# Group 11's reciprocal real gate: from two ScalarE steps to one GpSimd power

## The chip, the cores and the metric

The kernel runs on one NeuronCore of a Trainium2 chip. Its engines are TensorE (PE in the profile: matrix products), VectorE (DVE) and ScalarE (ACT) for work on tiles in the on-chip memory, GpSimd (POOL), which does simple tile work and issues small DMAs in software, and SyncE (SP), which issues the large loads, stores and transposing DMAs. Every engine works through its own queue in order; semaphores hold an instruction until what it reads is there. The metric is the time of one execution in microseconds (us) on the device, lower is better.

## The reference

The reference is a gated linear recurrence, followed by a gated feed-forward layer with a residual. The part that matters here is the complex gate `a_re + i a_im` of each time step, head and channel, which is scaled to a magnitude of at most 0.999:

```python
mag = np.sqrt(a_re * a_re + a_im * a_im)
scale = np.minimum(mag, 0.999) / (mag + 1e-06)
a_re_n, a_im_n = (a_re * scale, a_im * scale)
for t in range(S):
    ar, ai = a_re_n[:, :, t, :, None], a_im_n[:, :, t, :, None]
    new_re = ar * S_re - ai * S_im
    new_im = ar * S_im + ai * S_re
    S_re, S_im = (new_re + kv, new_im)
    y[:, :, t] = np.einsum('bhd,bhde->bhe', q[:, :, t], S_re)
```

`kv` is the outer product of k and v at step t. There are 4 batches, 8 heads, 768 steps and 48 channels. After it, `x = y` reshaped to 3072 x 384 goes through `x + sigmoid(x @ w_res) * ((gelu(x @ w_gate) * (x @ w_val)) @ w_out)`, with 1536 hidden columns.

## The kernel before, in words

The recurrence is turned into a chunked form. The 768 steps of each batch are cut into three stretches of 256, each of two chunks of 128 steps; a stretch of one batch is a **group**, and there are 12 groups (0 to 3 are the first stretch of the four batches, 4 to 7 the second, 8 to 11 the third). Steps lie on the 128 partitions, heads and channels along the row, 384 numbers for a chunk and 768 for a group.

For each group the gate becomes two running sums over time: that of the logarithm of the magnitude, and that of the phase. The phase of a gate is arctan(a_im / a_re). So the kernel needs a_im times the reciprocal of a_re, which it takes as the square of a_re to the power -1/2. Steps are named with the group behind them; for group 11 they run so:

- SQI11 and SQR11 (ScalarE): squares of a_im and a_re, the latter in place in tile `ar`.
- ADD11 (VectorE, L573): adds both squares into tile `m2`, capped. It reads `ar`.
- LNR11 and EXR11 (ScalarE, L577 and L578): logarithm of `ar` in place, then its exponential with a scale of -0.5: now `ar` holds 1/a_re.
- TH11 (VectorE, L554): `ai` = `ar` times `ai`. ATN11 (ScalarE) is its arctangent.
- CST11.c (TensorE, L631): running sum of the phases of a chunk as a product with a triangular matrix, in f32.

A chunk's running phase has to begin where the chunk before it ended. The last row of the reduced phase is multiplied by -2 pi into a row of a scratch tile `G` (CRA and CRB steps, L679), and a DMA with accumulation adds it to the first row of the next chunk's `ai` (CDA and CDB steps, L684; GpSimd issues them). CDB4 carries from group 4's second chunk to group 8's first, and **CST8.0 on TensorE reads that row**; OFF8.0 on ScalarE reads CST8.0's result. The other small GpSimd DMAs move rows of the magnitudes through DRAM so that the state of the recurrence can be scaled (DR at L582, DS at L585, DE and DI, DT at L611). GpSimd also does casts of v (VC, L520) and additions of the residual (RX, L874).

The feed-forward layer works on units of 256 or 512 rows: products with the gate and value weights (L837), gelu (ScalarE), their product (VectorE, L848), the residual gate (L852), the output product (L862), and the rest on VectorE, GpSimd and SyncE. PSUM accumulators of the products and of the running sums share four banks, named in the order.

The order of all work is written out by hand in `ORDER`, one list of about 1370 steps. Each step goes to one engine, and each engine's queue has its steps in the order of the list; nothing is rearranged when the kernel runs. The names `log`, `trig` and `gelu` in it load ScalarE's function tables.

In that list, on GpSimd, the steps around the change are RX3.1, then CDB4, DS8.1, DS9.1, DR10, DR11, DI8, CRA9, CDA9 and DT8.0. LNR11 stood between RX3.1 and CDB4 in the list, but on ScalarE's queue; EXR11 stood shortly before TH11.

Of the kernel before, what the change touches and what calls it, by code (L numbers as in the profile page):

```python
# [10 lines left out]
FP = mybir.dt.float32  # L11
# [3 lines left out]
OP = mybir.AluOpType  # L15
PSUM = bass.MemoryType.PSUM

PARAMS = {'units': [[0], [1], [2], [3], [4, 5], [6, 7], [8, 9], [10, 11]],
 'turn': 5,
 'wq': 4,  # L20
 'split': [0],
 'bufs': {'ar': 4,
          'ai': 6,
          'm2': 4,
          'q': 4,
          'k': 4,
# [235 lines left out]
        'XC4.0': 'ACT',  # L262
        'XC4.1': 'DVE'},
 'pairf': 1,
 'rat': []}

ORDER = """
# [46 lines left out]
DE6:1 GP4.0:2 Lai10.1 QT6:1 SQI11:1 SG4.3 GP4.3:3 VP4.11:1 GE4.3 SQR11 RX2.0 Lvf6.1:1 GE4.0 KR7 VP4.5:0 HM4.11 MM7:1  # L314
MN7 EN7 GP4.9:3 RP4.2:1 SQI10:2 DK6.0 SG4.2 GE4.9 HM4.5 ADD11 CSL9.0:211 VP4.3:0 ADD10 KT6:1 AT6.0.1:10 HM4.3 DS9.0:0
DE7:0 RX3.0 DS8.0:1 log EI9.0 CDB5 CSL8.0:100 CST9.0:3 AT6.0.0:01 EX9.0 CSL8.1:0 VC7.0:0 EX8.0 RX3.1 AM6.0.1 AM6.0.0
EI8.0 VC6.1 EX8.1 LNR11 CDB4 DS8.1 MI6:1 DS9.1 OFF9.0 CST8.0:2 DR10:0 ST2.0 DR11:1 DI8 Y6.0:3 FR9.0 AT6.1.1:10
AT6.1.0:01 AM6.1.1 DK6.1 ED6 EI8.1 AM6.1.0 OFF8.0 CRA9 CSL9.1:1 VP4.10:3 VP4.1:0 EI9.1 X6.0 ST3.0 Lvf7.1:0 EX9.1 LM10
LM11 ML8 LNR10 ML9 FR8.0 ME8 Y6.1:5 X6.1 EB7:0 EXR11 EXR10 QT7:0 HM4.10 HM4.1 KT7:0 AT7.0.1:10 AT7.0.0:01 CDA9 AM7.0.0
VP4.6:1 Lk10.0:3 Lq11.0:2 Lk8.0:2 VP4.0:2 VP4.9:3 VP4.8:0 HM4.6 AM7.0.1 HM4.0 CST9.1:1 HM4.9 OFF9.1 TH11 FR9.1 DT8.0:0  # L320
VP4.4:2 RP4.0:3 Y7.0:4 DK7.0 HM4.4 HM4.8 AT7.1.0:00 VC7.1 CRA8 CDA8 RP4.1:1 XD6.1:1 AT7.1.1:11 CST8.1:2 AM7.1.0 MI7:1
ST3.1 XD6.0 OFF8.1 FR8.1 AM7.1.1 OP4.0.0:0 trig ATN11 Lk8.1 Lvf8.1:1 X7.0 gelu SG4.0 Lq9.1:1 ABS9 OT4.0:2 Lvf9.0:0
# [56 lines left out]
def kernel(  # L379
# [13 lines left out]
    nc = tc.nc  # L393
    B, H, S, D = q.shape
    DD = 2 * D
    DM = H * D
# [15 lines left out]
    singles = ctx.enter_context(tc.tile_pool(name="singles", bufs=1))  # L412
# [4 lines left out]
    if PARAMS["rat"]:  # L417
        one = singles.tile([128, 1], FP, name="one")
        nc.vector.memset(one, 1.0)
    lmat, tmat = [], []  # L420
    for val, dst in ((1.0, lmat), (I2PI, tmat)):
        ut = singles.tile([128, 128], FP, name="ut%d" % (val == 1.0))
# [79 lines left out]
    def flat(t):  # L502
        return t.rearrange("p c h d -> p (c h d)") if len(t.shape) == 4 else t

    def part(key, cs):
        return flat(st[key])[:, cs[0] * DM:(cs[-1] + 1) * DM]

    def act(out, in_, func, **kw):
        return nc.scalar.activation(out=out, in_=in_, func=func, **kw)  # L509

    def on(name, default):
        return PARAMS["eo"].get(name, default)
# [14 lines left out]
    def gates(p):  # L527
        s = p // B
        split = p in PARAMS["split"]
        parts = [(0,), (1,)] if split else [(0, 1)]  # L530

        def each(nm, eng, f, r, w, table=None, whole=False):
            for cs in ([(0, 1)] if whole else parts):
                name = nm + str(p) + ("" if len(cs) > 1 else ".%d" % cs[0])
                e = on(name, eng)
                st.add(name, e, (lambda cs=cs, e=e: f(cs, e)) if nm in ("SQI", "SQR") else lambda cs=cs: f(cs),
                       r=[(n, p, c) for n in r for c in cs], w=[(n, p, c) for n in w for c in cs], table=table)
# [3 lines left out]
        def square(eng, o, i):  # L541
            if eng == "ACT":
                return act(o, i, AF.Square)
            return (nc.gpsimd if eng == "POOL" else nc.vector).tensor_tensor(out=o, in0=i, in1=i, op=OP.mult)
# [8 lines left out]
        def theta():  # L553
            each("TH", "DVE", lambda cs: nc.vector.tensor_tensor(  # L554
                out=part(("ai", p), cs), in0=part(("m2" if rat else ln, p), cs), in1=part(("ai", p), cs), op=OP.mult),
                ["m2" if rat else ln, "ai"], ["ai"])
        if rat:

            each("LNR", "ACT", lambda cs: act(part(("ar", p), cs), part(("ar", p), cs), AF.Ln), ["ar"], ["ar"], "log")
            each("EXR", "ACT", lambda cs: act(part(("m2", p), cs), part(("ar", p), cs), AF.Exp, scale=-1.0), ["ar"], ["m2"], "log")  # L560
            theta()
            each("SQI", sq[0], lambda cs, e: square(e, part(("m2", p), cs), part(("ai", p), cs)), ["ai"], ["m2"])
            each("LM", "ACT", lambda cs: act(part(("m2", p), cs), part(("m2", p), cs), AF.Ln, bias=one), ["m2"], ["m2"], "log")
            each("ADD", "DVE", lambda cs: nc.vector.scalar_tensor_tensor(
                out=part(("m2", p), cs), in0=part(("ar", p), cs), scalar=2.0, in1=part(("m2", p), cs), op0=OP.mult, op1=OP.add),
                ["m2", "ar"], ["m2"])
            each("MNL", "DVE", lambda cs: nc.vector.tensor_scalar(
                out=part(("m2", p), cs), in0=part(("m2", p), cs), scalar1=math.log(CAP), scalar2=math.log(1e-37),
                op0=OP.min, op1=OP.max), ["m2"], ["m2"])
        else:  # L570
            each("SQI", sq[0], lambda cs, e: square(e, part(("m2", p), cs), part(("ai", p), cs)), ["ai"], ["m2"])
            each("SQR", sq[1], lambda cs, e: square(e, part(("ar", p), cs), part(("ar", p), cs)), ["ar"], ["ar"])
            each("ADD", "DVE", lambda cs: nc.vector._custom_dve(  # L573
                TENSOR_ADD_SAT, out=part(("m2", p), cs), in0=part(("m2", p), cs), in1=part(("ar", p), cs), s0=CAP, s1=1e-37),
                ["m2", "ar"], ["m2"])
            if not split:
                each("LNR", "ACT", lambda cs: act(part(("ar", p), cs), part(("ar", p), cs), AF.Ln), ["ar"], ["ar"], "log")  # L577
                each("EXR", "ACT", lambda cs: act(part(("ar", p), cs), part(("ar", p), cs), AF.Exp, scale=-0.5),  # L578
                     ["ar"], ["ar"], "log")
            theta()  # L580
        if s > 0:
            st.add("DR%d" % p, "POOL", lambda: nc.gpsimd.dma_start(out=st["d1", p], in_=st["m2", p][0:1, 0:DM]),  # L582
                   r=[("m2", p, 0)], w=[("d1", p)])
            for u in range(2):
                st.add("DS%d.%d" % (p, u), "POOL", lambda u=u: nc.gpsimd.dma_start(  # L585
                    out=st["m1", p][u * D:(u + 1) * D], in_=st["d1", p].rearrange("r (h d) -> d (r h)", h=H)),
# [9 lines left out]
        for c in range(C):  # L596
            st.add("CSL%d.%d" % (p, c), "PE", lambda c=c: nc.tensor.matmul(  # L597
                out=st["csl", (p, c)], lhsT=lmat[c], rhs=part(("m2", p), (c,)), start=True, stop=True),
# [5 lines left out]
        if s < NS - 1:  # L604
            st.add("DE%d" % p, "POOL", lambda: nc.gpsimd.dma_start(
                out=st["d3", p + B][0:1, :], in_=st["E", p][127:128, DM:W]), r=[("E", p, 1)], w=[("d3", p + B, 0)])
        if s > 0:
            st.add("DI%d" % p, "POOL", lambda: nc.gpsimd.dma_start(
                out=st["d3", p][1:2, :], in_=st["Ei", p][0:1, 0:DM]), r=[("Ei", p, 0)], w=[("d3", p, 1)])
            for u in range(2):  # L610
                st.add("DT%d.%d" % (p, u), "POOL", lambda u=u: nc.gpsimd.dma_start(  # L611
                    out=st["m3", p][u * D:(u + 1) * D].rearrange("p r h -> p (r h)"),
# [3 lines left out]
                out=st["M", p][0:DD], in0=st["m3", p][0:DD, 0], in1=st["m3", p][0:DD, 1], op=OP.mult),  # L616
                r=[("m3", p)], w=[("M", p)])
            st.add("MN%d" % p, mne, lambda: engine(mne).tensor_tensor(  # L618
                out=st["M", p][0:DD], in0=st["M", p][0:DD], in1=st["m1", p][0:DD], op=OP.mult),
                r=[("M", p), ("m1", p)], w=[("M", p)])  # L620

        for c in range(C):
            cs = (c,)
# [10 lines left out]
            if on("OFF%d.%d" % (p, c), "ACT") == "ACT":  # L634
# [4 lines left out]
                    out=part(("m2", p), cs), in0=part(("m2", p), cs), scalar=MAGIC, in1=st["cst", (p, c)],  # L639
                    op0=OP.subtract, op1=OP.subtract), r=[("cst", (p, c)), ("m2", p, c)], w=[("m2", p, c)])  # L640
            else:
                st.add("OFF%d.%d" % (p, c), "DVE", lambda cs=cs, c=c: nc.vector.tensor_scalar(
                    out=part(("m2", p), cs), in0=st["cst", (p, c)], scalar1=MAGIC, scalar2=MAGIC, op0=OP.add,
                    op1=OP.subtract), r=[("cst", (p, c))], w=[("m2", p, c)])
                st.add("FR%d.%d" % (p, c), "DVE", lambda cs=cs, c=c: nc.vector.tensor_tensor(
                    out=part(("m2", p), cs), in0=part(("m2", p), cs), in1=st["cst", (p, c)], op=OP.subtract),
                    r=[("cst", (p, c)), ("m2", p, c)], w=[("m2", p, c)])
        if s < NS - 1:
# [3 lines left out]
            out=part(("ai", p), cs).bitcast(I32), in0=part(("m2", p), cs).bitcast(I32), scalar1=0x7FFFFFFF, scalar2=None,  # L652
# [272 lines left out]
    for p in range(NG):  # L925
        gates(p)
# [44 lines left out]
```

## Time and profile before

| what | value |
|---|---|
| median of 2 runs | 274.96 us (273.47 to 276.45) |
| the profiled execution | 273.17 us |
| its span, first to last instruction | 271.4 us |
| busy: TensorE, VectorE, ScalarE, GpSimd | 233.4, 222.3, 213.4, 104.9 us |
| mean granted TensorE clock | 0.965 |

The span is what the profile sees; 1.8 us of the execution lie around it. Busy time is the time in which an engine worked on tiles; waiting, and the issue of SP's DMAs, do not count. TensorE's busy time is modelled from the instructions' sizes. In the lines of the profile a tile is named by its program name: several groups share names, `m` stands for tiles `m1`, `m2` and `m3`, `d` for the DRAM tiles. An arrow points from what is read to what is written (`ar<-ar`).

### The profile page before, as it was taken

How to read it: one execution, taken by the hardware profiler on the slowest of the kernel's cores; microseconds unless marked ns; L12 is line 12 of the kernel's file. 1: busy time of each engine (PE TensorE's matmuls, PEld its weight loads, DVE VectorE, ACT ScalarE, POOL GpSimd, SP SyncE). 2: the span in 40 equal slices, each digit the busy share in tenths (PEclk: the TensorE clock that was granted, in tenths of full speed). 3: DMA queues.
4: the chain of work that ended last, by engine and by line, in shares of the span. 5: the costliest groups of instructions: out<-in, count | busy, mean ns of one | idle time of the engine just before them, and what ended most of it. 6: DMA issues, size and time to landing. Idle time of an engine off the chain costs nothing.

```text
span 271.4 us, 5296 instructions
## 1 busy us (share of the span) xinstructions
PE 233.4 (86%) x1914; PEld 146.5 (54%) x1926; DVE 222.3 (82%) x370; ACT 213.4 (79%) x340; POOL 104.9 (39%) x149
## 2 busy tenths in 40 slices
PE   0455576997989989999997999999999999999993
PEld 0112444784767677677743566645566455654461
DVE  0746989988899999999999999988988999533633
ACT  3799999897899999989998799979969982225420
POOL 4000291632315989254487156404940611130000
PEclk9995759999999999999999999999999999999998
DMA  7999999999994899998979966994975694521002
GB/s 151 207 205 201 210 190 185 184 184 192 178 207 86 167 163 192 198 186 159 197 149 198 213 118 110 184 175 98 187 134 134 127 170 103 89 87 58 2 29 87
DMA packets 170714, 41.35 MB, mean 152 GB/s; under 512 B 162624, under 2 KB 170688, under 8 KB 170688
## 3 DMA queue, kind: packets, MB, share of 16 engines
q1 hardware_dynamic: 163200, 37.04, 69.1%
q0 software_dynamic: 7488, 3.97, 11.6%
q8 instruction: 15, 0.25, 0.4%
q14 instruction: 11, 0.09, 0.1%
HBM read 31.33 MB, written 4.76 MB: 133 GB/s over the span
## 4 chain that ended last, share of the span: by engine, by line
PE 40%; DVE 21%; DMA 15%; issue 13%; ACT 8%; POOL 1%; SPq 1%; DVEq 0%; POOLq 0%
PE gv L837 20%; PE sums L862 6%; DMA wo<-in_moe_w_out_dram 3%; PE sums L631 3%; DVE h L848 3%; DMA d<-m 3%; PE sums L597 3%; PE sums L852 3%; DMA wv<-in_moe_w_val_dram 3%; DMA KT<-padK 2%; PE at L748 2%; ACT L938 2%; ACT CS L509 2%; DVE atm L751 2%; DVE m L573 2%
## 5 line engine op out<-in xcount | busy, mean ns | idle before, releaser
L837 PE MATMUL gv<-xT,wv 128*128 128x256 bf16 (+1 forms) x281 | 54.7, 324 | 3.2 <-DVE h L848 2.1
L848 DVE SCALAR_TENSOR_TENSOR h<-h,gv 128x512 bf16<-128x512 bf16 x72 | 47.4, 681 | 12.0 <-PE gv L837 11.7
L509 ACT ACTIVATE h<-gv 128x512 bf16<-128x512 f32 x72 | 40.7, 599 | 21.0 <-PE gv L837 20.3
L837 PE MATMUL gv<-xT,wg 128*128 128x256 bf16 (+1 forms) x283 | 53.7, 325 | 2.4 <-DMA out_dram<-ot 0.6
L862 PE MATMUL sums<-wo,h 128*128 128x384 bf16 x288 | 49.4, 326 | 1.5 <-DMA wo<-in_moe_w_out_dram 1.5
L938 ACT ACT_TABLE_LOAD x37 | 47.5, 1283 | 1.4 <-PEq L955 0.7
L837 PEld LDWEIGHTS <-wv 128*128 128x128 bf16 x288 | 27.1, 97 | 22.3 <-issue 5.5
L837 PEld LDWEIGHTS <-wg 128*128 128x128 bf16 x288 | 27.2, 97 | 21.0 <-issue 2.8
L862 PEld LDWEIGHTS <-h 128*128 128x128 bf16 x288 | 27.6, 98 | 19.7 <-issue 2.4
L751 DVE TENSOR_TENSOR atm<-at,mask 128x512 bf16<-128x512 f32 x48 | 32.1, 681 | 1.2 <-PE at L748 1.1
L509 ACT ACTIVATE ar<-ar 128x768 f32<-128x768 f32 x31 | 25.6, 847 | 0.1
L631 PE MATMUL sums<-ai,ut 128*128 128x384 f32 x40 | 19.2, 569 | 6.5 <-ACT ai L509 5.8
L867 DVE SCALAR_TENSOR_TENSOR ot<-sg,sums 128x384 f32<-128x384 f32 x24 | 12.9, 548 | 13.9 <-PE sums L862 10.5
L520 POOL CAST v<-vf 128x384 bf16<-128x384 f32 x13 | 12.8, 981 | 24.6 <-DMA vf<-in_v_dram 24.4
L597 PE MATMUL sums<-m,ut 128*128 128x384 f32 x24 | 11.2, 550 | 10.9 <-ACT m L509 10.3
L684 POOL DMA_DIRECT2D ai<-G x16 | 14.1, 887 | 13.1 <-DVE G L679 6.5
L509 ACT ACTIVATE sg<-sums 128x384 f32<-128x384 f32 x24 | 11.6, 496 | 8.3 <-PE sums L852 7.7
L585 POOL DMA_DIRECT2D m<-d x16 | 11.8, 772 | 12.9 <-DVE M L618 7.5
L611 POOL DMA_DIRECT2D m<-d x16 | 13.0, 817 | 7.7 <-DMA d<-Ei 7.7
L852 PE MATMUL sums<-wr,xT 128*128 128x384 bf16 x72 | 15.1, 325 | 0.4 <-DVE h L848 0.4
L679 POOL TENSOR_SCALAR G<-m 32x384 f32<-32x384 f32 x8 | 11.3, 1414 | 7.7 <-issue 5.9
L796 PE MATMUL y<-v,atm 128*128 128x48 bf16 x192 | 12.4, 185 | 2.2 <-DVE atm L751 1.9
(94 smaller groups left out, 453.0 us busy)
## 6 DMA issues: line engine op xcount, KB each, us to landing
ar<-in_a_re_dram SPq DMA_DIRECT2D x24, 192.0 KB, 3.8
ai<-in_a_im_dram SPq DMA_DIRECT2D x24, 192.0 KB, 3.8
vf<-in_v_dram SPq DMA_DIRECT2D x24, 192.0 KB, 3.7
k<-in_k_dram SPq DMA_DIRECT2D x24, 192.0 KB, 4.2
q<-in_q_dram SPq DMA_DIRECT2D x24, 192.0 KB, 4.0
out_dram<-ot SPq DMA_DIRECT2D x24, 192.0 KB, 2.6
wv<-in_moe_w_val_dram POOLq DMA_DIRECT2D x4, 288.0 KB, 11.0
wg<-in_moe_w_gate_dram POOLq DMA_DIRECT2D x4, 288.0 KB, 10.4
```

The source lines that it names most:

```text
L509: return nc.scalar.activation(out=out, in_=in_, func=func, **kw)
L597: st.add("CSL%d.%d" % (p, c), "PE", lambda c=c: nc.tensor.matmul(out=st["csl", (p, c)], lhsT=lmat[c], rhs=part(("m2", p), (c,)), start=Tru ...
L611: st.add("DT%d.%d" % (p, u), "POOL", lambda u=u: nc.gpsimd.dma_start(out=st["m3", p][u * D:(u + 1) * D].rearrange("p r h -> p (r h)"), in_ ...
L631: return r + [nc.tensor.matmul(out=o, lhsT=tmat[c if s == 0 else 1], rhs=part(("ai", p), (c,)), start=not both, stop=True)]
L684: st.add("CD%s%d" % (nm, p), "POOL", lambda: nc.gpsimd.dma_start(out=part(("ai", pn), (cn,))[0:1], in_=row[127:128], accum_op=OP.add), r=[ ...
L751: st.add("AM" + sfx, "DVE", lambda: nc.vector.tensor_tensor(out=st["atm", i], in0=st["at", i], in1=mask4, op=OP.mult), r=[("at", i)], w=[( ...
L837: st.add("%sP%d.%d" % (nm.upper(), u, f), "PE", lambda f=f, fs=fs, nm=nm, w=w: [nc.tensor.matmul(out=st[nm + "p", (u, f)][:, j * 256:j * 2 ...
L848: st.add("HM%d.%d" % (u, f), "DVE", lambda f=f, h2=h2: nc.vector.scalar_tensor_tensor(out=h2(), in0=h2(), scalar=0.5, in1=gv(("vp", (u, f) ...
L852: st.add("RP%d.%d" % (u, jj), "PE", lambda jj=jj: [nc.tensor.matmul(out=st["rp", (u, jj)], lhsT=st["xT", u][:, i, jj * 128:(jj + 1) * 128] ...
L862: st.add("OP%d.%d.%d" % (u, jj, hh), "PE", lambda jj=jj, fs=fs: [nc.tensor.matmul(out=st["op", (u, jj)], lhsT=st["h2", u][:, f, jj * 128:( ...
L867: st.add("OT%d.%d" % (u, jj), "DVE", lambda jj=jj: nc.vector.scalar_tensor_tensor(out=st["ot", (u, jj)], in0=st["sg", u][:, jj], scalar=1. ...
L938: nc.scalar.preload_act_table_set(tables[nm])
```

## The change

One setting, `pow`, lists the groups whose reciprocal is taken by GpSimd; it holds group 11 alone. For that group LNR11 and EXR11 are left out, and a step PW11 on GpSimd takes `ar` to the power of a tile of -0.5, one column of it spread over all 768, in one instruction. PW11 stands in the order where LNR11 stood: GpSimd comes to it after RX3.1 and before CDB4. The tile of -0.5 is filled by VectorE once, in the preparation. All other steps stay in their places.

```diff
+ 'pow': [11],
...
-EI8.0 VC6.1 EX8.1 LNR11 CDB4 DS8.1 MI6:1 DS9.1 OFF9.0 CST8.0:2 DR10:0 ST2.0 DR11:1 DI8 Y6.0:3 FR9.0 AT6.1.1:10
+EI8.0 VC6.1 EX8.1 PW11 CDB4 DS8.1 MI6:1 DS9.1 OFF9.0 CST8.0:2 DR10:0 ST2.0 DR11:1 DI8 Y6.0:3 FR9.0 AT6.1.1:10
...
-LM11 ML8 LNR10 ML9 FR8.0 ME8 Y6.1:5 X6.1 EB7:0 EXR11 EXR10 QT7:0 HM4.10 HM4.1 KT7:0 AT7.0.1:10 AT7.0.0:01 CDA9 AM7.0.0
+LM11 ML8 LNR10 ML9 FR8.0 ME8 Y6.1:5 X6.1 EB7:0 EXR10 QT7:0 HM4.10 HM4.1 KT7:0 AT7.0.1:10 AT7.0.0:01 CDA9 AM7.0.0
...
+    mhalf = singles.tile([128, 16], FP, name="mhalf")
+    nc.vector.memset(mhalf, -0.5)
+    mhalf = mhalf[:, 0:1]
...
-            if not split:
+            if p in PARAMS["pow"]:
+                each("PW", "POOL", lambda cs: nc.gpsimd.tensor_tensor(
+                    out=part(("ar", p), cs), in0=part(("ar", p), cs), in1=mhalf.to_broadcast([128, len(cs) * DM]), op=OP.pow),
+                    ["ar"], ["ar"])
+            elif not split:
```

## The prediction

> **What bounds the kernel now.** I read the page first, then the busy time by stretch from the place of the change to the end, then TensorE's waits there.
>
> ```profile
> span 271.4 us, 5296 instructions
> ...
> PE 233.4 (86%) x1914; PEld 146.5 (54%) x1926; DVE 222.3 (82%) x370; ACT 213.4 (79%) x340; POOL 104.9 (39%) x149
> ```
> ```profile
> 150.00:157.00 7.00, 6.59 (x39) 3.68 (x39) 6.46 (x10) 4.99 (x10) 1.15 (x3) 1.00 1.07 207
> 157.00:160.00 3.00, 2.95 (x40) 1.92 (x39) 2.97 (x7) 2.79 (x7) 1.66 (x3) 1.00 0.94 179
> 160.00:170.00 10.00, 10.00 (x97) 6.11 (x96) 9.73 (x17) 9.94 (x19) 6.37 (x10) 1.00 0.52 92
> 170.00:180.00 10.00, 9.35 (x73) 5.29 (x73) 9.32 (x15) 9.02 (x13) 3.10 (x4) 1.00 0.91 177
> 250.00:260.00 10.00, 9.95 (x51) 4.88 (x51) 5.86 (x9) 4.34 (x8) 0.00 (x0) 1.00 0.01 2
> ```
> ```profile
> PE gv L837 <- DMA out_dram<-ot: 0.6, 1, 0.6
> PE y L796 <- POOL v L520: 0.2, 1, 0.2
> PE gv L837 <- DVE ot L867: 0.2, 1, 0.2
> ```
>
> The columns of the second view are the stretch, its length, then the busy time of PE, PE's weight loads, DVE, ACT and POOL, the granted clock and the DMA share. From 157 us TensorE is busy for 9.35 to 10 of every 10 us, at the full clock, and the third view lists all that it waits for from 157 us to the end: 1.0 us. The page's chain of waits names 9.9 us of "issue" behind a GpSimd cast at 226 us, but TensorE is busy through it. So in this part TensorE sets the end. A delay of TensorE has nowhere to be made up, and ScalarE work that is taken away shortens nothing by itself.
>
> **The place of the change.** GpSimd's queue there, in order of time (start, length):
>
> ```profile
> 145.52 1.26 POOL L874 TENSOR_TENSOR ot<-ot,x 128x384 f32<-128x384 f32 x1
> 146.38 1.15 POOL L684 DMA_DIRECT2D ai<-G  x1
> 147.09 1.77 POOL L585 DMA_DIRECT2D m<-d  x2
> 154.54 1.02 POOL L582 DMA_DIRECT2D d<-m  x2 [5.68 <-DVE m L573]
> 156.87 0.49 POOL L608 DMA_DIRECT2D d<-Ei  x1 [1.31 <-DVE atm L751]
> ```
>
> These are RX3.1, CDB4, DS8.1 with DS9.1, DR10 with DR11, and DI8. PW11 goes between the first two. It writes `ar` in place, which ADD11 reads, so it can't start before ADD11 is done. The answer for ADD11's line in this stretch, then for CDB4's issue, and the matmul that reads what CDB4 brings (the second pair of f32 sums there, CST8.0):
>
> ```profile
> L573 DVE CUSTOM_DVE_ANT_0 m<-m,ar x2: 952/953/954, 152.4 to 153.3; 128x768 f32<-128x768 f32 x2
> ```
> ```profile
> DMA to landing us min/median/max: 3.3/3.3/3.3
> ```
> ```profile
> 156.54 0.81 PE L631 MATMUL sums<-ai,ut 128*128 128x384 f32 x2
> ```
>
> CDB4 was issued at 146.38 and landed 3.3 us later, at 149.7: 6.8 us before CST8.0 wanted it. Now it stands behind PW11.
>
> **Part 1, the wait.** ADD11 runs from 152.43 to 153.38. GpSimd answers VectorE 0.29 us later (ADD10 ends at 154.25, DR10 starts at 154.54), so PW11 starts at 153.67. With P for its time, CDB4 is issued at 153.67 + P, and lands 2.0 us (the quickest of these carries behind 157 us, in the stretch with the DMA share of 0.52) to 3.3 us (its own row) later; I take 2.6, since the loads behind it will have drained. CST8.0 starts at 156.27 + P instead of 156.54: TensorE stands for **P - 0.3 us**. This is a new wait in the place of none, and it is not paid from 0: the 7 us that GpSimd waits for ADD11 have eaten the slack before the power begins.
>
> All others stop with it. Behind CST8.0 on TensorE are Y6.0, the attention products of group 6 and group 4's value products; VectorE and ScalarE wait for those (the mask at L751, OFF8.0 at 158.34 in ScalarE's queue). Behind PW11 on GpSimd, DS8.1, DS9.1, DR10, DR11, DI8, CRA9 and CDA9 follow CDB4 back to back: by their rows 1.8 + 1.0 + 0.5 + 1.2 + 0.8 us, so CDA9 is issued 6 us after CDB4 and lands 2 to 3 later, some 8.5 us after the power's end. CST9.1, which reads it, came 7.2 us after CST8.0 (163.70), which is now 9.8 us after the power's end. So they are not late a second time. TH11 came at 164.47, 7.9 us after CST8.0; the power is done before CST8.0 and costs TH11 nothing.
>
> **Part 2, the power's time P.** No row shows a power. The nearest by form and engine, from GpSimd's groups by shape, and the answer for its casts:
>
> ```profile
> L874 POOL TENSOR_TENSOR ot<-ot,x 128x384 f32<-128x384 f32 x12 | 11.6, 968 | 5.0 <-DVE ot L867 4.8
> L615 POOL TENSOR_TENSOR M<-m 96x8 f32<-96x8 f32 x5 | 1.3, 263 | 3.3 <-DMA m<-d 3.3
> ```
> ```profile
> L520 POOL CAST v<-vf x5: 504/582/3848, 145.0 to 236.1; 128x384 bf16<-128x384 f32 x5
> ```
>
> The floor: a power as one arithmetic step, two operands in, 968 ns for 384 columns, so 1.94 us for 768. The steps: a power of any two numbers is a logarithm, a product and an exponential, each to f32 accuracy a polynomial with range reduction; I count 18 arithmetic steps as my estimate, 36 with two-word care and special cases. The price of a step: the two-operand addition costs 968 - 504 = 464 ns more than the cast, 1.2 ns a column for one more operand and one step, 0.93 us for 768 columns. 18 steps at this and the pass of a cast (1.0 us) give 17.7 us. The ceiling: 18 steps at a whole two-operand pass each, 18 x 1.94 = 35 us. A second reading falls between: the tiny 96x8 product takes 263 ns for 8 columns, 33 ns a column, 25 us if every column paid that. I take **P = 17 us**, near the step count at the marginal price, and keep 1.94 and 35 as the ends. This is the weakest term of the sum.
>
> **Part 3, the clock.** TensorE's clock fell to half in idle stretches before 41 us. The stretch from 33 us was granted 0.50 with TensorE 2.7 of 4.3 us busy; it took 3.4 us of full work until 40.7 us to come back:
>
> ```profile
> 33.00:37.30 4.30, 2.70 (x29) 2.22 (x27) 3.70 (x7) 4.29 (x6) 2.84 (x4) 0.50 1.03 192
> 37.30:40.70 3.40, 3.40 (x6) 1.58 (x6) 3.20 (x5) 3.37 (x5) 3.40 (x6) 0.53 1.21 186
> ```
>
> After standing 17 us TensorE should resume at half speed for about 3.4 us, which loses half of it: **+1.7 us** (0 to 3.4).
>
> **Part 4, what is removed.** Two ScalarE passes of 0.75 us between starts (the `ar<-ar` rows at 157.23 and 163.56). No table load goes with them: the exponentials of groups 8 and 9 and LNR10, EXR10 use the same table. ScalarE is not what TensorE waits for behind 157 us: **0**; were it, at most -1.5. The wait of 0.6 us for a store's DMA may vanish, since stores drain in the stand: **-0.6**. The fill of the -0.5 tile is one VectorE instruction of some 0.06 us (its neighbours' rows) in VectorE's idle 5.2 us ahead of its first tile work at 6.13 us: 0.
>
> **VectorE beside the power.** The casts' row shows that GpSimd and VectorE hold each other up: 504 ns alone, 3848 at worst. [...]
>
> **The sum**: 16.7 (P - 0.3) + 1.7 - 0.6 = 17.8 us. On the profiled execution's 273.17 us that is 291.0; on the median, 1.8 us higher, 292.8. I give **292**. In general the median becomes 274.96 + P + 0.8. A measurement of this kernel tells about 2%, 5.5 us, from no change, and P reaches that near 5 us.
>
> **The rivals.**
> - **A cheap power**, under 5 us: GpSimd does it nearly as it does an addition. TensorE then stands 1.6 us or less at P = 1.94, too short for the clock: 276 to 277, 280 at most. Not slower by 2%. For it: the form is that of an ordinary two-operand instruction, the nearest row by form. Against it: ScalarE needs two table passes for the same value. **0.11**.
> - **A dear power**, over 35 us: the steps of a column wait for each other and columns don't overlap. 36 steps at a whole pass each are 70 us, 346 us in all. For it: even the addition costs 2.5 ns a column, twice the cast. Against it: that row already has a price of 1.2 ns for a step. [...] **0.14**.
> - **The carry gets past the power**: DMA issues on GpSimd overlap the tile work ahead of them (CDB4 begins at 146.38, RX3.1 ends at 146.78). If CDB4 ran beside the power, TH11 alone would wait: at P = 17 until 170.7 instead of 164.47, 6 us, 281 in all. Against it: the overlap seen is 0.4 us. **0.03**.
> - The forecast, P from 5 to 35 and TensorE behind it: **0.71**, 281 to 311. Faster by over 2% needs a gain of 5.5 us, where ScalarE gives up 1.5 and isn't waited for: 0.01.
>
> The range takes in the forecast, the cheap power and the carry past it, and so both ends of P: **276 to 311**; the dear power, 0.14, is outside. Faster 0.01, same 0.11, slower 0.88 (forecast, dear power and the carry past it).
>
> **What would show it.** One GpSimd instruction on `ar`, 128x768, of about 17 us, starting at 153.7 behind a wait for L573. An idle time of TensorE of the same size less 0.3 us ahead of one f32 sums matmul, released by the DMA `ai<-G`, and half the granted clock for 3 to 4 us behind it. From there to the end the spacing of before. The prediction is wrong if P is outside 5 to 35 us, if the gap is released by something else, or if TensorE's stretches behind it get shorter.

## The result: 44% slower, by the power's own time

| | before | after |
|---|---|---|
| median | 274.96 us | 395.76 us (395.58 to 395.95, 2 runs) |
| ratio | | 1.4417, 95% interval 1.4338 to 1.4495 |
| span of the profiled execution | 271.4 us | 393.8 us |

I forecast 292 us with a range of 276 to 311. The direction was right and the size was far off. From the page of the kernel after, the lines on engines, on slices of the span and on groups of instructions (busy time, mean ns of one, idle time ahead and what ended it):

```profile
span 393.8 us, 5308 instructions
...
PE 237.2 (60%) x1926; PEld 149.5 (38%) x1926; DVE 222.4 (56%) x371; ACT 212.0 (54%) x338; POOL 228.7 (58%) x150
...
PE   0657898998999986000000000000799999999995
...
POOL 3024452259944555999999999999841560411200
PEclk9955699999999999555555555555799999999999
...
L581 POOL TENSOR_TENSOR ar<-ar,mhalf 128x768 f32<-128x768 f32 x1 | 123.3, 123346 | 6.7 <-DVE m L577 6.7
...
L639 PE MATMUL sums<-ai,ut 128*128 128x384 f32 x40 | 20.0, 590 | 127.9 <-DMA ai<-G 122.1
```

One GpSimd instruction takes 123.3 us. The busy times of TensorE and VectorE are nearly those of before, so almost all that was added is standing: the zeros in TensorE's row fall in the same slices as the nines in GpSimd's. GpSimd's queue around the power (start, length), the same steps that were shown of before:

```profile
144.29 1.28 POOL L882 TENSOR_TENSOR ot<-ot,x 128x384 f32<-128x384 f32 x1
152.26 123.35 POOL L581 TENSOR_TENSOR ar<-ar,mhalf 128x768 f32<-128x768 f32 x1 [6.69 <-DVE m L577]
275.58 0.81 POOL L692 DMA_DIRECT2D ai<-G  x1
276.21 1.52 POOL L593 DMA_DIRECT2D m<-d  x2
277.53 1.22 POOL L590 DMA_DIRECT2D d<-m  x2
278.53 0.69 POOL L616 DMA_DIRECT2D d<-Ei  x1
```

The order is as told: RX3.1, a wait of 6.7 us for ADD11, the power, then CDB4, DS8.1 and DS9.1, DR10 and DR11, DI8. CDB4's landing, the matmul that waits for it, and the busy times by stretch (length, then PE, weight loads, DVE, ACT, POOL, granted clock, DMA) at the restart:

```profile
DMA to landing us min/median/max: 1.9/1.9/1.9
```
```profile
277.63 1.62 PE L639 MATMUL sums<-ai,ut 128*128 128x384 f32 x2 [122.14 <-DMA ai<-G]
```
```profile
160.00:270.00 110.00, 0.00 (x0) 0.00 (x0) 0.00 (x0) 0.00 (x0) 110.00 (x1) 0.50 0.00 0
277.50:281.00 3.50, 3.37 (x35) 2.61 (x36) 0.64 (x1) 0.58 (x1) 3.13 (x6) 0.52 0.09 7
281.00:291.00 10.00, 10.00 (x95) 5.89 (x94) 9.91 (x18) 9.02 (x17) 6.02 (x8) 1.00 0.27 55
```

From 160 to 270 us no engine but GpSimd does anything, the DMA engines included. CST8.0 then runs at half the clock (1.62 us for the pair of f32 matmuls, 0.81 before), and the full clock is back at 281 us.

The 122.4 us of span come out of three marks. ADD11 began 1.2 us earlier in this execution than in that of before (151.23 against 152.43), so CST8.0 was due at 155.34: **-1.2**. It started at 277.63: **+122.3**. From there to the end it took 116.2 us, against 114.9 from 156.54 before: **+1.3**.

### The profile page after: what moved, and what is told of

Its sections match the earlier page's. It is cut to its first block, busy times and chain, and to the rows that moved or that the text cites. A ratio compares the mean times of both kernels' runs of the same rounds, so it can differ in the third digit from the quotient of the medians.

```text
span 393.8 us, 5308 instructions
## 1 busy us (share of the span) xinstructions
PE 237.2 (60%) x1926; PEld 149.5 (38%) x1926; DVE 222.4 (56%) x371; ACT 212.0 (54%) x338; POOL 228.7 (58%) x150
## 3 DMA queue, kind: packets, MB, share of 16 engines
q0 software_dynamic: 7488, 3.97, 7.5%
## 4 chain that ended last, share of the span: by engine, by line
issue 35%; PE 30%; DVE 13%; DMA 11%; ACT 8%; POOL 1%; SPq 1%; DVEq 0%; POOLq 0%; ACTq 0%
PE gv L845 15%; PE sums L870 5%; PE sums L639 2%; DMA wo<-in_moe_w_out_dram 2%; ACT L946 2%; DVE h L856 2%; DMA d<-m 2%; PE sums L860 2%; ACT CS L513 2%; PE sums L605 2%; DMA wv<-in_moe_w_val_dram 2%; PE at L756 2%; DMA KT<-padK 1%; DVE atm L759 1%; ACT ai L513 1%
## 5 line engine op out<-in xcount | busy, mean ns | idle before, releaser
L581 POOL TENSOR_TENSOR ar<-ar,mhalf 128x768 f32<-128x768 f32 x1 | 123.3, 123346 | 6.7 <-DVE m L577 6.7
L639 PE MATMUL sums<-ai,ut 128*128 128x384 f32 x40 | 20.0, 590 | 127.9 <-DMA ai<-G 122.1
L513 ACT ACTIVATE m<-sums,magic 128x384 f32<-128x384 f32 x9 | 5.2, 575 | 126.2 <-PE sums L639 126.1
L639 PEld LDWEIGHTS sums<-ai,ut 128*128 128x128 f32 x40 | 7.2, 214 | 131.7 <-issue 123.4
L845 PE MATMUL gv<-xT,wv 128*128 128x256 bf16 (+1 forms) x288 | 54.9, 325 | 2.9 <-DVE h L856 2.2
L845 PE MATMUL gv<-xT,wg 128*128 128x256 bf16 (+1 forms) x288 | 54.1, 325 | 2.1 <-DVE xT L524 0.6
L845 PEld LDWEIGHTS <-wv 128*128 128x128 bf16 x288 | 27.2, 98 | 22.1 <-issue 5.5
L845 PEld LDWEIGHTS <-wg 128*128 128x128 bf16 x288 | 27.2, 97 | 20.9 <-issue 2.8
L513 ACT ACTIVATE ar<-ar 128x768 f32<-128x768 f32 x29 | 23.9, 840 | 0.1
L605 PE MATMUL sums<-m,ut 128*128 128x384 f32 x24 | 12.3, 601 | 11.2 <-ACT m L513 10.0
```

Of the source, the lines that this page charges most:

```text
L581: each("PW", "POOL", lambda cs: nc.gpsimd.tensor_tensor(out=part(("ar", p), cs), in0=part(("ar", p), cs), in1=mhalf.to_broadcast([128, len ...
L639: return r + [nc.tensor.matmul(out=o, lhsT=tmat[c if s == 0 else 1], rhs=part(("ai", p), (c,)), start=not both, stop=True)]
L845: st.add("%sP%d.%d" % (nm.upper(), u, f), "PE", lambda f=f, fs=fs, nm=nm, w=w: [nc.tensor.matmul(out=st[nm + "p", (u, f)][:, j * 256:j * 2 ...
```

## The experiments

The question was what the 123 us are made of, whether they act through GpSimd's queue alone, and whether the rest of the sum holds at the size that I had assumed. One more run, a power in GpSimd's idle time, raised a question of its own, which four further runs answered.

### A multiplication in the power's place

```diff
-                    out=part(("ar", p), cs), in0=part(("ar", p), cs), in1=mhalf.to_broadcast([128, len(cs) * DM]), op=OP.pow),
+                    out=part(("ar", p), cs), in0=part(("ar", p), cs), in1=mhalf.to_broadcast([128, len(cs) * DM]), op=OP.mult),
```

> The power is replaced by a multiplication of the same form, operands and place (so the gate of group 11 is wrong: it is -0.5 times the square). Theory: the 123.35 us of the power are the operation's own arithmetic, and the rest of the change costs next to nothing. Then this GpSimd instruction takes about 1.9 us, TensorE's gap ahead of the f32 sums matmul is 1 to 3 us instead of 122, and the time is 275 to 278 us. Rival: the form is what is dear (an operand spread from one column, or GpSimd being held up by VectorE for the whole operation). Then the multiplication takes over 100 us too, and the time stays near 390.

Measured: 275.79 us median, ratio 1.0031 (1.0000 to 1.0062). The instruction, and of TensorE's waits behind 150 us the one for the carry:

```profile
L581 POOL TENSOR_TENSOR ar<-ar,mhalf x1: 2117/2117/2117, 154.2 to 154.2; 128x768 f32<-128x768 f32 x1
```
```profile
PE sums L639 <- DMA ai<-G: 1.6, 1, 1.6
```

The form, the spread operand and the place cost 2.1 us of GpSimd and a wait of 1.6 us. The other 121 us are the power's. This is also the cheap rival played out: its price was 276 to 277.

### The power of 96 columns, the rest on ScalarE

```diff
-                    out=part(("ar", p), cs), in0=part(("ar", p), cs), in1=mhalf.to_broadcast([128, len(cs) * DM]), op=OP.pow),
-                    ["ar"], ["ar"])
+                    out=part(("ar", p), cs)[:, 0:96], in0=part(("ar", p), cs)[:, 0:96], in1=mhalf.to_broadcast([128, 96]), op=OP.pow),
+                    ["ar"], ["ar"])
+                each("LNR", "ACT", lambda cs: act(part(("ar", p), cs)[:, 96:], part(("ar", p), cs)[:, 96:], AF.Ln), ["ar"], ["ar"], "log")
+                each("EXR", "ACT", lambda cs: act(part(("ar", p), cs)[:, 96:], part(("ar", p), cs)[:, 96:], AF.Exp, scale=-0.5),
+                     ["ar"], ["ar"], "log")
```

In the order LNR11 is back, right behind PW11, and EXR11 in its old place.

> The power is taken of the first 96 columns alone; ScalarE takes logarithm and exponential of the other 672. Theory: the time goes by columns, 123.35 / 768 = 160.6 ns each. Then the power takes 15.4 us, and by the prediction's formula (274.96 + P + 0.8) the time is 291 us (288 to 294), with a TensorE gap of some 15 us in front of the same matmul. Rival: most of the 123 us is paid once, at the first use of the operation. Then the power still takes over 100 us and the time is 375 to 395.

Measured: 289.84 us median, ratio 1.0583 (1.0506 to 1.0660). The same two views:

```profile
L581 POOL TENSOR_TENSOR ar<-ar,mhalf x1: 16318/16318/16318, 153.4 to 153.4; 128x96 f32<-128x96 f32 x1
```
```profile
PE sums L642 <- DMA ai<-G: 15.1, 1, 15.1
```

An eighth of the columns takes 16.3 us, not over 100, so there is no large cost of first use. This run is also close to the prediction as I made it: a power of 16.3 us instead of my 17, though ScalarE keeps its two passes. The formula, 274.96 + P + 0.8, gives 292.1; with the before of these runs (274.61), 291.7. Measured 289.84. Everything in the sum but P was good to 2 us.

### The carry ahead of the power

```diff
-EI8.0 VC6.1 EX8.1 PW11 CDB4 DS8.1 MI6:1 DS9.1 OFF9.0 CST8.0:2 DR10:0 ST2.0 DR11:1 DI8 Y6.0:3 FR9.0 AT6.1.1:10
+EI8.0 VC6.1 EX8.1 CDB4 DS8.1 MI6:1 DS9.1 PW11 OFF9.0 CST8.0:2 DR10:0 ST2.0 DR11:1 DI8 Y6.0:3 FR9.0 AT6.1.1:10
```

> The whole power, but CDB4, DS8.1 and DS9.1 are issued ahead of it. Theory: GpSimd's queue is what holds all others, and the next thing wanted from it is CDA9, 7.2 us later on TensorE. Then CST8.0 has no gap, TensorE stands in front of CST9.1 instead, from about 162.5 us until the power's end at 275.6 us and the 5.5 us of issue and landing of the five steps behind it: 118.6 us, for a time of 392 us against 395.8. Rival: only the carry into group 8 mattered and nothing else is held but the reader of the power, TH11 on VectorE, from 163.3 until 275.7 us: 112 us, for a time of 387.

Measured: 393.21 us median. TensorE's f32 sums of phases between 150 and 285 us, and its largest wait:

```profile
154.48 0.81 PE L639 MATMUL sums<-ai,ut 128*128 128x384 f32 x2
156.05 0.81 PE L639 MATMUL sums<-ai,ut 128*128 128x384 f32 x2
281.41 1.62 PE L639 MATMUL sums<-ai,ut 128*128 128x384 f32 x2 [118.03 <-DMA ai<-G]
```

CST8.0 now follows at once (156.05), and the gap stands in front of CST9.1: 118.0 us where 118.6 were expected. TH11, the reader of the power, stood as well; who waited for the power (us, times):

```profile
  DVE ai L558: 112.3, 1
```

But the power, which TH11 waited for, ended at 276.32 (152.98 + 123.34), and TensorE went on only at 281.41, when the next carry, CDA9, had landed. In both orders the size of the gap is set by the first carry that TensorE wants from behind the power in GpSimd's queue.

### A row of powers behind the last step

Behind the last step, on tiles that nobody reads any more (shortened; `gp` is one GpSimd operation on two operands, `spread` takes one column for all):

```diff
+        gp(8, bx[:, 0:8], spread(by, 8), OP.pow)
+        gp(32, bx[:, 0:32], spread(by, 32), OP.pow)
+        gp(96, bx, spread(by, 96), OP.pow)
+        gp(16, bx[:, 0:16], by, OP.pow)
+        gp(16, bx[0:32, 0:16], by[0:32], OP.pow, parts=32)
+        gp(32, bx[:, 0:32], spread(bz, 32), OP.pow)
+        gp(96, bx, spread(by, 96), OP.mult)
+        for i, nm in enumerate(("two", "copy", "psum")):
...
+            nc.gpsimd.tensor_copy(out=z, in_=bx[:, 0:8])
+            gp(96, bx, spread(by, 96), OP.pow)
...
+                nc.vector.tensor_tensor(out=d, in0=bx, in1=by[:, 0:1].to_broadcast([128, 96]), op=OP.mult)
```

> The kernel before, and behind its last step a row of GpSimd operations on idle tiles: powers of 8, 32 and 96 columns to -0.5, 16 columns with an operand that isn't spread, the same on 32 of 128 partitions, 32 columns to the power 1.0, a multiplication of 96 columns; then three powers of 96 columns, each beside one VectorE operation: a product of two tiles in on-chip memory, a copy, and a product of one such tile and one PSUM tile. Theory, arithmetic by columns: 1.3, 5.1 and 15.4 us, 2.6 and 2.6 us, 5.1 us, and about 0.25 us for the multiplication; so the time is some 75 us above that of before. Rival, a cost of first use: the first power takes over 100 us and the others are short. Rival, the spread operand: the 16 columns without it take under 0.3 us. Rival, special values: the power to 1.0 is much shorter. Beside the power: if a GpSimd operation excludes VectorE operations with two operands in on-chip memory for its whole time, the first of the three products starts only at its power's end, 15 us late, and the third doesn't; if not, all three run at once in under 0.3 us.

Measured: 333.64 us in one run, 59 us above before and not some 75: GpSimd began the row at 246.9 us, while TensorE still had work until 270 us. GpSimd's groups by shape, then its timeline at the end of the row:

```profile
L955 POOL TENSOR_TENSOR E<-bx,by 128x32 f32<-128x32 f32 x1 | 5.4, 5408 | 0.0
L955 POOL TENSOR_TENSOR E<-bx,bz 128x32 f32<-128x32 f32 x1 | 5.4, 5405 | 0.0
L955 POOL TENSOR_TENSOR E<-bx,by 128x16 f32<-128x16 f32 x1 | 2.9, 2890 | 0.0
L955 POOL TENSOR_TENSOR E<-bx,by 32x16 f32<-32x16 f32 x1 | 2.9, 2888 | 0.0
L955 POOL TENSOR_TENSOR E<-bx,by 128x8 f32<-128x8 f32 x1 | 1.7, 1680 | 0.0
```
```profile
280.66 0.34 POOL L955 TENSOR_TENSOR E<-bx,by 128x96 f32<-128x96 f32 x1
280.95 0.18 POOL L968 COPY m<-bx 128x8 f32<-128x8 f32 x1
281.10 15.62 POOL L955 TENSOR_TENSOR E<-bx,by 128x96 f32<-128x96 f32 x1
```

From 32 to 96 columns the time grows by 15.62 - 5.41 = 10.21 us, 159.5 ns a column, with some 0.3 us once; on that line 768 columns take 122.8 us, and 123.35 were measured. The number of partitions (32 or 128) and the exponent (-0.5 or 1.0) change nothing. Nor does the spread of the operand, as far as this goes: the 16 columns have a full second operand, and their 2.9 us lie on the line of the others, which have it spread. The multiplication of 96 columns takes 0.34 us, a 46th. VectorE beside the first and the last of the three powers:

```profile
281.38 0.24 DVE L972 TENSOR_TENSOR m<-bx,by 128x96 f32<-128x96 f32 x1
...
312.83 0.24 DVE L976 TENSOR_TENSOR m<-bx,sums 128x96 f32<-128x96 f32 x1
```

The product of two tiles in on-chip memory ran 0.28 us after the power began and took 0.24 us, as the one with a PSUM operand did. A power that is under way doesn't hold these VectorE operations.

### What ScalarE's relief is worth

```diff
-EI8.0 VC6.1 EX8.1 LNR11 CDB4 DS8.1 MI6:1 DS9.1 OFF9.0 CST8.0:2 DR10:0 ST2.0 DR11:1 DI8 Y6.0:3 FR9.0 AT6.1.1:10
+EI8.0 VC6.1 EX8.1 CDB4 DS8.1 MI6:1 DS9.1 OFF9.0 CST8.0:2 DR10:0 ST2.0 DR11:1 DI8 Y6.0:3 FR9.0 AT6.1.1:10
...
-LM11 ML8 LNR10 ML9 FR8.0 ME8 Y6.1:5 X6.1 EB7:0 EXR11 EXR10 QT7:0 HM4.10 HM4.1 KT7:0 AT7.0.1:10 AT7.0.0:01 CDA9 AM7.0.0
+LM11 ML8 LNR10 ML9 FR8.0 ME8 Y6.1:5 X6.1 EB7:0 EXR10 QT7:0 HM4.10 HM4.1 KT7:0 AT7.0.1:10 AT7.0.0:01 CDA9 AM7.0.0
```

> The kernel before without LNR11 and EXR11, and nothing in their place (group 11's gate is left as the square of its real part, so its phases are wrong): what ScalarE's relief is worth by itself. Theory: TensorE sets the end behind 157 us, so two ScalarE passes less are worth nothing: ratio 0.997 to 1.003. Rival: ScalarE's place in the chain pays them out, 1.5 us: ratio 0.994 or less.

Measured: ratio 1.0009 (0.9976 to 1.0041). To leave both ScalarE passes out altogether gains nothing that can be measured: by the interval at most 0.24%. In this order of work, no way of computing this reciprocal elsewhere had more than that to win.

### A short operation that keeps nothing waiting

The multiplication again, in the place that the power had behind the carry:

```diff
-EI8.0 VC6.1 EX8.1 PW11 CDB4 DS8.1 MI6:1 DS9.1 OFF9.0 CST8.0:2 DR10:0 ST2.0 DR11:1 DI8 Y6.0:3 FR9.0 AT6.1.1:10
+EI8.0 VC6.1 EX8.1 CDB4 DS8.1 MI6:1 DS9.1 PW11 OFF9.0 CST8.0:2 DR10:0 ST2.0 DR11:1 DI8 Y6.0:3 FR9.0 AT6.1.1:10
```

> The multiplication in the power's place (group 11's gate is -0.5 times the square), but behind CDB4, DS8.1 and DS9.1 on GpSimd. Theory: the 0.85 us that the multiplication in front of CDB4 cost is the wait of CST8.0 for the carry, 1.6 us of TensorE. Issued ahead, the carry is in time, the 2.1 us delay only CDA9, which has some slack: no gap ahead of CST8.0, under 1 us ahead of CST9.1, ratio 0.998 to 1.002. Rival: any tile work of GpSimd there costs VectorE the time, by shared access to the on-chip memory; then the ratio stays near 1.003 or above though no gap is left.

Measured: ratio 0.9976 (0.9948 to 1.0004), and no wait of TensorE for the carry is left. That fits the wait of 1.6 us as the price of the multiplication ahead of CDB4; at 0.3% that price is hardly clear of the noise.

### A power in GpSimd's idle time

```diff
+    bx = singles.tile([128, 40], FP, name="bx")
+    nc.vector.memset(bx, 0.72)
+    by = singles.tile([128, 16], FP, name="by")
+    nc.vector.memset(by, -0.5)
...
+    st.T["bx", 0] = bx
+    st.add("PB", "POOL", lambda: nc.gpsimd.tensor_tensor(
+        out=bx, in0=bx, in1=by[:, 0:1].to_broadcast([128, 40]), op=OP.pow), w=[("bx", 0)])
...
-CDB6 MM9:0 log
+CDB6 PB MM9:0 log
```

> The kernel before, with its ScalarE steps, and one more GpSimd instruction: a power of 40 columns on an idle tile whose result nobody reads, behind CDB6, where GpSimd waits 7.5 us (176.7 to 184.2 us) for VectorE anyway. Theory: a power costs the kernel what it keeps waiting in GpSimd's queue and nothing else. By 160 ns a column it takes 6.6 us, fits into the idle time, and the ratio is 0.997 to 1.003. Rival: a running power slows the work of VectorE, which is busy for 8 of 10 us there, or its memory accesses; then the products with two operands in on-chip memory in that stretch (950 ns each) get longer and the ratio is 1.005 to 1.02.

Measured: ratio 1.0084 (1.0051 to 1.0117). That seemed to speak against the theory. But in the trace the power took 7.42 us inside the idle time, and the steps ahead of it were 2.1 us late already. So the next run left the power out and kept the two tiles:

```diff
-CDB6 PB MM9:0 log
+CDB6 MM9:0 log
```

> The run before (power of 40 columns in GpSimd's idle time) without its power: only its two small tiles and their two fills at the start are left. In that run's trace the lateness of 2.1 us was there before the power began (the product into ai for group 10 at 174.17 instead of 172.03 us). Theory: the tiles or fills cost it, not the power: ratio 1.005 to 1.012, like that run's 1.0084. Rival: the power cost it and the early lateness was scatter of one profile: ratio 0.997 to 1.003.

Measured: ratio 1.0123 (1.0082 to 1.0163) with no power at all. And the other way round, the power without new tiles:

```diff
+    st.T["bx", 0] = tmat[0]
+    st.add("PB", "POOL", lambda: nc.gpsimd.tensor_tensor(
+        out=tmat[0][:, 0:40], in0=magic.to_broadcast([128, 40]), in1=hpi.to_broadcast([128, 40]), op=OP.pow), w=[("bx", 0)])
...
-CDB6 MM9:0 log
+CDB6 PB MM9:0 log
```

> The same power of 40 columns in the same place, but without new tiles: it reads two constants that are there and writes into a triangular matrix that is no longer read. Theory: a power costs the kernel what it keeps waiting in GpSimd's queue and nothing else; it takes 6.6 to 7.4 us, ends inside GpSimd's idle time, and the ratio is 0.997 to 1.003. Rival: the power slows VectorE or the memory: ratio 1.005 to 1.012.

Measured: ratio 1.0000 (0.9980 to 1.0020). GpSimd's queue there, and two of VectorE's products with two operands in on-chip memory beside the power:

```profile
176.48 7.42 POOL L926 TENSOR_TENSOR lt<-magic,hpi 128x40 f32<-128x40 f32 x1
184.53 0.71 POOL L585 DMA_DIRECT2D m<-d  x1 [0.62 <-DVE M L618]
```
```profile
179.36 0.96 DVE L696 TENSOR_TENSOR kE<-k,Ei 128x768 bf16<-128x768 f32 x1 [0.77 <-DMA k<-in_k_dram]
...
182.43 0.96 DVE L696 TENSOR_TENSOR qE<-q,E 128x768 bf16<-128x768 f32 x1
```

A power of 7.4 us that ends before its queue is wanted again (0.62 us of waiting are left behind it) costs nothing that can be measured, and the products beside it have their usual 0.96 us.

### The two small tiles

That left the 1.2% of two tiles that nobody uses. Two runs tell the fills from the place of the tiles. Two more fills and no tile:

```diff
+    nc.vector.memset(hpi, -0.5 * math.pi)
...
+    nc.vector.memset(magic, MAGIC)
```

> The kernel before with two more VectorE fills at the start, of tiles that are there already; no tile is added. It tells the fills from the place of the tiles, as the cause of the 1.2% that two small unused tiles (160 and 64 bytes a partition) cost. In that run's trace the loads took longer to land (4.6 against 3.8 us for ar) and the hardware queue's packets had 80% of the DMA engines' span against 69%. Theory, the place: all tiles behind the two are shifted by 224 bytes and the loads' targets with them, so the fills alone cost nothing: ratio 0.997 to 1.004, landing 3.8 us. Rival, the fills delay the start: ratio 1.008 or more, landing 3.8 us.

Measured: ratio 0.9980 (0.9944 to 1.0015). The two tiles with 256 bytes a partition instead of 224:

```diff
-    bx = singles.tile([128, 40], FP, name="bx")
+    bx = singles.tile([128, 48], FP, name="bx")
...
```

> The two unused tiles and their fills, but 192 and 64 bytes a partition, 256 together instead of 224. Theory: what costs is that all tiles behind them no longer start at a multiple of 64 bytes; 256 keeps that: ratio 0.997 to 1.004, landing 3.8 us, queue share 69%. Rival: any shift of the tiles costs it: ratio 1.008 to 1.015, landing 4.6 us, share 80%.

Measured: ratio 0.9997 (0.9965 to 1.0029). The row of the hardware queue (packets, MB, share of the DMA engines' span) and the loads of `ar` (KB each, median us to landing), first with 224 bytes, then with 256:

```profile
q1 hardware_dynamic: 163200, 37.04, 80.1%
...
ar<-in_a_re_dram SPq DMA_DIRECT2D x24, 192.0 KB, 4.6
```
```profile
q1 hardware_dynamic: 163200, 37.04, 69.0%
...
ar<-in_a_re_dram SPq DMA_DIRECT2D x24, 192.0 KB, 3.7
```

The same packets and bytes take 80 instead of 69% of the DMA engines' span, and a load of `ar` lands 0.9 us later. The fills alone do nothing (0.9980), and two tiles of 256 bytes do nothing (0.9997). What is left as the cause is that everything behind the two tiles is shifted by 224 bytes; that is a conclusion from these runs, no trace shows a tile's address. Why that shift should slow the loads stays open. The 0.8% of the run with the power and the two tiles are then the tiles': the power alone gave 1.0000, the tiles alone 1.0123.

## Why the prediction was wrong, and where it was right

- **What bounds the kernel: right.** From 157 us the end is TensorE's. Without the two ScalarE passes the time is 1.0009 (0.9976 to 1.0041) of before, and TensorE's gap of 122.3 us is found in a span that is 122.4 us longer.
- **Part 1, the wait: right in its mechanism and nearly in size.** The power started behind ADD11, CDB4 stood behind it, and CST8.0 waited for the carry. I put the gap at P - 0.3; it was P - 1.2 (122.1 with P = 123.35, and 15.1 with 16.32). CDB4 landed in 1.9 us where I took 2.6, and GpSimd answered ADD11 in 0.08 us (152.18 to 152.26) where I took 0.29. Behind the 2.1 us of multiplication CST8.0 started 2.76 us after CDB4 began to be issued (156.28 to 159.04), behind the power 2.05 (275.58 to 277.63), and there the gap was P - 0.5 (1.59 with 2.12). That the rest of the queue causes no second gap was right too: TensorE waits for no GpSimd DMA behind 282 us.
- **Part 2, the power's time: the step that failed.** I counted 18 arithmetic steps, an estimate of how a power is computed that no run shows, and priced each at what an addition costs above a cast, 1.2 ns a column; that gave 17 us, with 35 as the ceiling. Measured: 159.5 ns a column, 123.3 us. Per column this is 133 of my steps. The error was to take the price of a step of a power from rows that hold one step at most, an addition and a cast: nothing in them says that a power is made of such steps. How much of the factor of 7 is the count of steps and how much the price of one, no run tells. The tiny 96x8 product (33 ns a column) was no bound either, since a short instruction is dear per column without being a power: a copy of 8 columns took 0.18 us, 22 ns a column, and a multiplication of 96 columns 0.34 us, 3.5 ns a column. With no row near the thing, the ceiling of 35 was not a bound, and the range should have been left open above.
- **The rivals.** The dear power (0.14) came true in its condition, P over 35 us, and even that was priced at 70 us. I had let its 0.14 go as the part outside the range. Its mechanism, columns that don't overlap and steps that wait for each other, is not shown. What the runs do show is that columns add up (159.5 ns each) and partitions don't (2.89 us for 16 columns on 32 and on 128), and that neither the exponent (5.41 us for 32 columns at -0.5 and at 1.0) nor its form matters (16 columns with a full second operand, 2.89 us, lie on the line of the spread ones, 2.85). The cheap power, played with a multiplication, gave 1.0031, as priced, and its wait of 1.59 us was too short for the clock: the pair of f32 matmuls behind it took 0.88 us, not 1.62. That the carry gets past the power is refuted: CDB4 was issued at the power's end.
- **Part 3, the clock: right.** Half the clock for 3.3 us behind the stand. The first gate product behind CST8.0 (L845, L837 of before) came 3.97 us after it instead of 2.43: 1.5 us lost at the restart, against +1.7. Of the -0.6 for the store's wait not all came: it vanished, but two other waits (0.5 and 0.3 us) took its place. Together I had put it at +1.1 us; the stretch from CST8.0 to the end got 1.3 longer.
- **Part 4, the removed passes: right,** at 0, within the interval given above. Both pages, before and after, have 37 table loads on ScalarE.
- **VectorE beside the power.** The casts of before fit the two engines holding each other up. GpSimd's of 3.85 us began with a row of VectorE operations, most of them on two operands in on-chip memory (213.61), and ended 0.36 us behind the last (217.10); the one of 504 ns was not alone, as I wrote, but beside operations with one operand in PSUM (162.50). A VectorE cast (L520, 96x384) took 2.23 us beside GpSimd's cast and RX3.1 and ended 0.22 us behind RX3.1 (146.78); its like at 219.96 us took 0.35. With the power one direction was seen. A power that began while VectorE worked on two operands in on-chip memory was longer by about what was left of that operation: 16.32 us instead of 15.62 for 96 columns, 0.70 more, with 0.7 to 0.8 of ADD10 to go (begun at 153.2, 0.95 long, the power from 153.41); 7.42 for 40 columns instead of some 6.7, my estimate from 159.5 ns a column and 0.3 us once, with 0.77 to go (176.48 to 177.25). The other direction was not: once a power ran, VectorE's products started at once (0.28 us into it) and were no longer for it: 0.24 us for 96 columns with two operands in on-chip memory as with one in PSUM, and 0.96 us for 768 columns, as in before.

## What to carry to other kernels

Where the trace has no row of an operation, the nearest row by form gives a floor and no ceiling: forecast as a function of the unknown time, name the point from which it decides, and leave the range open above, or ask for one measurement of a short piece first (a power of 8 columns, 1.68 us, would have told: 0.21 us a column). An instruction costs what it keeps waiting behind it in its engine's queue: 7.4 us of power in idle time cost nothing here, and 2.1 us of multiplication ahead of a carry cost 1.6 us of TensorE. And ask first what the relief is worth: here, on ScalarE, nothing that could be measured, so that a replacement had next to nothing to win; none of the runs beats the kernel before by more than its interval.

## What the runs showed of the hardware that I had not expected

- A power on GpSimd costs 159.5 ns a column of f32, the same on 32 partitions as on 128 (16 columns: 2.89 us on both). For 96 columns it takes 46 times as long as a multiplication (15.62 us against 0.34).
- Two small unused tiles in front of all others cost 1.2%: with 224 bytes a partition loads of `ar` landed in 4.6 us and the time was 1.0123 (1.0082 to 1.0163) of before, with 256 in 3.7 us and 0.9997 (0.9965 to 1.0029). The kernel with the row of powers, whose tiles took 480 bytes, also had its `ar` loads land in 4.6 us; the change itself, whose tile takes 64, in 3.7. So of the four sizes the two multiples of 64 bytes landed early and the two odd multiples of 32 late; other sizes were not tried.
